# A fused attention and mixing kernel: every engine's order planned by a list scheduler, mixing as filler, long-row loads, V cast on chip

## The chip, the cores and the metric

The kernel runs on one core of a Trainium2 chip. The metric is the device time of one execution in microseconds (us). Beside the timed runs, one execution of each kernel was profiled (span and mean granted clock are on record for every run); its *span* runs from the first to the last instruction and is some 1 to 3 us shorter than the timed runs. Engines: PE does matmuls and transposes, PEld is its weight loading, DVE is the vector engine, ACT the scalar engine, POOL the general engine, SP issues DMA.

## The reference, cut to what matters

Four batches of eight heads, 768 positions, head size 64. Each query sees the three blocks of 64 keys with the best gate score (query times mean key of the block), plus its own block, causally. The attention output goes through a token mixing and a channel mixing.

```python
k_rep = k.reshape(B, H, n_blocks, 64, D).mean(axis=3)
gate_scores = einsum('bhsd,bhnd->bhsn', q, k_rep)            # causal blocks only
mask = top-3 blocks of each query, plus its own block, and causal
attn = softmax(where(mask, q @ k.T / sqrt(D), -1e9)) @ v
x = attn.transpose(0, 2, 1, 3).reshape(B, S, 512)
u = x + (relu(x.T @ w_tok1) @ w_tok2).T                       # token mixing
out = u + relu(u @ w_ch1) @ w_ch2                             # channel mixing
```

In the first tile of 128 queries a query has at most two causal blocks, so top-3 selects all of them: the gates of tile 0 decide nothing.

## The kernel before

Heads are handled in 16 *pairs*, four to a batch. A pair needs: q and k loaded, transposed on PE (fp32) and copied out by ACT; block sums of k and the gate on DVE and PE; the mask, transposed by PE and put beside q; scores, exponential (ACT), multiplication with the diagonal mask (DVE); the product with V ("av") and its normalisation (DVE). When the four pairs of a batch are done, its mixing can run. Each function emits the work of all engines together, and the order of these calls is a fixed interleaving:

```python
preps[0]["trq"](); preps[0]["trk"](); preps[0]["gate"]()
preps[1]["trq"](); preps[0]["mask"](); preps[1]["trk"]()
...
    order = [scores(i, 0, 0)] + stage("gate", i + 1)
    order += [last_av] if last_av else []
    order += [scores(i, 0, 1)] + stage("trq", i + 2) + [scores(i, 0, 2), scores(i, 1, 0)]
    order += stage("mask", i + 1) + [av(i, 0), scores(i, 1, 1)] + stage("trk", i + 2)
    if i + 3 < NP:
        order.append(lambda: load(i + 3))
    order.append(scores(i, 1, 2))
    # the last batch's mixing ("pend") is shared out evenly over the calls of the next four pairs
```

Loads of q and k read one head as rows of 64 fp32 numbers (256 B); V is loaded and converted to fp16 by a DMA that POOL issues:

```python
nc.sync.dma_start(out=t[:, :, 64*g:64*g+64], in_=src[b, h+g].rearrange("(j p) d -> p j d", p=128))
nc.gpsimd.dma_start(out=V16[r][:, g, :, 0:64], in_=v[b, h+g].rearrange("(j p) d -> p j d", p=128))
```

The softmax here doesn't subtract the row's maximum and nothing guards it: scores larger than these inputs give would overflow.

Of the kernel before, what the change touches and what calls it, by code (L numbers as in the profile page):

```python
# [22 lines left out]
WHERE = {kk: (g, off) for g, (_, parts) in enumerate(GROUPS) for kk, off, _ in parts}  # L23


@with_exitstack
def kernel(
# [21 lines left out]
    MASKV = -30000.0  # L49

    sp = ctx.enter_context(tc.tile_pool(name="sb", bufs=1))
    pp = ctx.enter_context(tc.tile_pool(name="ps", bufs=1, space=bass.MemoryType.PSUM))

# [5 lines left out]
    def big(name):  # L59
        return pp.tile([128, 1024], FP, tag="big", bufs=2, name=name)  # L60

    def bank(shape, name, dtype=FP):
        return pp.tile(shape, dtype, tag="bank", bufs=3, name=name)

    pairs = [(b, h) for b in range(B) for h in range(0, H, 2)]
    NP = len(pairs)

    loads = {}

    def load(i):  # L70
        b, h = pairs[i]
        q32 = sp.tile([128, NJ, 128], FP, tag="q32", bufs=3, name=f"q32_{i}")
        k32 = sp.tile([128, NJ, 128], FP, tag="k32", bufs=3, name=f"k32_{i}")
        for t, src in ((q32, q), (k32, k)):
            for g in range(2):
                nc.sync.dma_start(out=t[:, :, 64 * g:64 * g + 64],
                                  in_=src[b, h + g].rearrange("(j p) d -> p j d", p=128))
        r = i % (R + 1)
        for g in range(2):
            nc.gpsimd.dma_start(out=V16[r][:, g, :, 0:64],  # L80
                                in_=v[b, h + g].rearrange("(j p) d -> p j d", p=128))
        loads[i] = (q32, k32)

    R = 3
# [5 lines left out]

    load(0)
    ident32 = const("id32", np.eye(128, dtype=np.float32), FP, nc.scalar)
    for r in range(R):
        nc.vector.memset(ks2[r], 0.0)
        nc.vector.memset(bn16[r], 0.0)
        nc.vector.memset(QA[r][0][64:128, :], 0.0)
        nc.vector.memset(QA[r][1][0:64, :], 0.0)
    for r in range(R + 1):
        nc.vector.memset(V16[r][:, :, :, 64:65], 1.0)
    pidx = np.arange(128)  # L100
    nidx = np.arange(NB)
    jidx = np.arange(NJ)
    mrow = 2 * jidx[None, :, None] + (pidx[:, None, None] >= 64)
    gb1 = (-1.0e6 * np.maximum(0, nidx[None, None, :] - mrow)).astype(np.float32)
    own1 = np.where(nidx[None, None, :] == mrow, 0.0, MASKV).astype(np.float32)
    gbias = const("gbias", np.concatenate([gb1, gb1], axis=2), FP, nc.scalar)
    own = const("own", np.concatenate([own1, own1], axis=2), FP, nc.scalar)
    ident16 = const("id16", np.eye(128, dtype=np.float16), F16, nc.scalar)
    m0_np = (np.arange(128)[None, :] >= np.arange(128)[:, None]).astype(np.float16)
    m0 = const("m0", np.stack([m0_np, m0_np], axis=1), F16, nc.scalar)  # L110
    ind_np = (np.arange(S)[None, :] // 64 == nidx[:, None]).astype(np.float16)
    ind64 = np.zeros((64, S), np.float16)
    ind64[0:NB] = ind_np
    ind_dram = nc.inline_tensor(ind64, name="indc").ap()
    for r in range(R):
        for x in range(2):
            lo = 64 if x == 0 else 0
            nc.sync.dma_start(out=KA[r][x][lo:lo + 64, :], in_=ind_dram)
        if r == 0:
            load(1)  # L120

# [3 lines left out]
    wc2_16 = sp.tile([128, NFC, DM], F16, tag="wc2", name="wc2")  # L125

    def weight_loads():
        w1 = moe_w_tok1.rearrange("(j p) t -> p j t", p=128)
        w2 = moe_w_tok2.rearrange("(g p) s -> p g s", p=128)
        c1 = moe_w_ch1.rearrange("(c p) f -> p c f", p=128)  # L130
        c2 = moe_w_ch2.rearrange("(g p) c -> p g c", p=128)
        th = [lambda: nc.gpsimd.dma_start(out=w1_16, in_=w1), lambda: nc.gpsimd.dma_start(out=w2_16, in_=w2)]
        th += [lambda c=c: nc.gpsimd.dma_start(out=wc1_16[:, c, :], in_=c1[:, c, :]) for c in range(NCC)]
        th += [lambda f=f: nc.gpsimd.dma_start(out=wc2_16[:, f:f + 3, :], in_=c2[:, f:f + 3, :])
               for f in range(0, NFC, 3)]
        return th

    xs = {}

    def prep(i):  # L140
        r = i % R
        st = {}

        def trq():
            q32 = loads[i][0]
            ps = big("tq")
            for j in range(NJ):
                nc.tensor.transpose(out=ps[:, 128 * j:128 * j + 128], in_=q32[:, j, :], identity=ident32)  # L148
            qt = sp.tile([128, S], FP, tag="qt", bufs=2, name=f"qt_{i}")
            nc.scalar.copy(out=qt, in_=ps[:, 0:S])  # L150
            st["qt"] = qt
            nc.gpsimd.tensor_copy(out=QA[r][0][0:64, :], in_=qt[0:64, :])
            nc.gpsimd.tensor_copy(out=QA[r][1][64:128, :], in_=qt[64:128, :])

        def trk():
            k32 = loads[i][1]
            ps = big("tk")
            for j in range(NJ):
                nc.tensor.transpose(out=ps[:, 128 * j:128 * j + 128], in_=k32[:, j, :], identity=ident32)  # L159
            kt = sp.tile([128, S], FP, tag="kt", bufs=2, name=f"kt_{i}")  # L160
            nc.scalar.copy(out=kt, in_=ps[:, 0:S])  # L161
            kst = sp.tile([128, NB], FP, tag="kst", bufs=2, name=f"kst_{i}")
            nc.vector.tensor_reduce(out=kst, in_=kt.rearrange("p (n w) -> p n w", w=64),
                                    axis=AX.X, op=ALU.add)
            nc.vector.tensor_copy(out=ks2[r][64:128, 0:NB], in_=kst[64:128, :])
            nc.vector.tensor_copy(out=ks2[r][0:64, NB:2 * NB], in_=kst[0:64, :])
            nc.gpsimd.tensor_copy(out=KA[r][0][0:64, :], in_=kt[0:64, :])
            nc.gpsimd.tensor_copy(out=KA[r][1][64:128, :], in_=kt[64:128, :])

        def gate():  # L170
            gps = bank([128, NJ, 2 * NB], "gps")
            for j in range(NJ):
                nc.tensor.matmul(out=gps[:, j, :], lhsT=st["qt"][:, 128 * j:128 * j + 128],  # L173
                                 rhs=ks2[r], start=True, stop=True)
            gm = sp.tile([128, NJ, 2 * NB], FP, tag="gm", bufs=2, name=f"gm_{i}")
            m8 = sp.tile([128, NJ, 2, 8], FP, tag="m8", bufs=2, name=f"m8_{i}")
            lt = sp.tile([128, NJ, 2 * NB], FP, tag="lt", bufs=2, name=f"lt_{i}")
            nc.vector.tensor_tensor(out=gm, in0=gps, in1=gbias, op=ALU.add)
            for j in range(NJ):
                for x in range(2):  # L180
                    nc.vector.max(out=m8[:, j, x, :], in_=gm[:, j, NB * x:NB * x + NB])
            nc.vector.tensor_tensor(
                out=lt.rearrange("p j (x n) -> p j x n", n=NB),
                in0=gm.rearrange("p j (x n) -> p j x n", n=NB),
                in1=m8[:, :, :, 2:3].broadcast_to([128, NJ, 2, NB]), op=ALU.is_lt)
            nc.vector.scalar_tensor_tensor(out=lt, in0=lt, scalar=MASKV, in1=own, op0=ALU.mult, op1=ALU.max)
            nc.vector.tensor_copy(out=bn16[r][:, :, :, 0:NB], in_=lt.rearrange("p j (x n) -> p j x n", n=NB))

        def mask():
            bps = bank([128, S], "bps", F16)  # L190
            for j in range(NJ):
                nc.tensor.transpose(out=bps[:, 128 * j:128 * j + 128],  # L192
                                    in_=bn16[r][:, j, :, :].rearrange("p x n -> p (x n)"), identity=ident16)
            nc.vector.tensor_copy(out=QA[r][0][64:64 + NB, :], in_=bps[64:64 + NB, :])  # L194
            nc.vector.tensor_copy(out=QA[r][1][0:NB, :], in_=bps[0:NB, :])

        return dict(trq=trq, trk=trk, gate=gate, mask=mask)

    E = {}

    def scores(i, x, g):
        r = i % R

        def f():
            width, parts = GROUPS[g]
            ps = big("sps")
            for kk, off, nq in parts:
                q0 = 128 * kk
                a = 0
                while a < nq:  # L210
                    n = min(nq - a, 512 - (off + a) % 512)
# [10 lines left out]
        return f  # L222

    def av(i, x):
        b, h = pairs[i]

        def f():
            aps = pp.tile([128, NJ, 65], FP, tag="av", bufs=1, name="aps")
# [93 lines left out]
    pend = []  # L322
# [35 lines left out]
    for _, g in pend:  # L358
        g()
# [30 lines left out]
```

## Time and profile before

| | before |
|---|---|
| time, median | 318.5 us in the first three runs (317.2 to 322.5) |
| span | 316.6 us |
| first scores / first mixing matmul | 28.8 / 81.2 us |
| busy: PE, DVE, ACT, POOL | 280.0, 181.9, 141.4, 86.6 us |

The first lines of the page of the kernel before: the busy time of each engine, then PE, granted clock and DMA in 40 equal slices of the span (tenths; 9 is 90% or more).

```profile
span 316.6 us, 5878 instructions
...
PE 280.0 (88%) x2272; PEld 182.0 (57%) x2272; DVE 181.9 (57%) x624; ACT 141.4 (45%) x185; POOL 86.6 (27%) x110
...
PE   1325888888999999999999999999999999899994
...
PEclk9999598778899999999999999999999999999999
DMA  9999999675444445646324444330000011100022
```

PE is nearly always busy from a quarter of the span on, and mostly idle before. DMA shows the opposite. The table of stretches cuts the execution at the first scores and at the first mixing matmul (columns: stretch, its length, then busy us and instruction count of PE, PEld, DVE, ACT, POOL, then granted PE clock, DMA share, GB/s):

```profile
0.00:28.80 28.80, 9.28 (x43) 7.92 (x44) 8.63 (x37) 3.68 (x4) 13.60 (x22) 1.00 1.20 196
28.80:81.20 52.40, 43.96 (x382) 32.43 (x381) 35.57 (x146) 30.84 (x37) 27.28 (x34) 0.80 1.07 151
81.20:316.60 235.40, 226.75 (x1851) 141.70 (x1848) 137.71 (x442) 106.92 (x145) 45.69 (x56) 1.00 0.29 58
```

In the 28.8 us head PE works 9.3 us. In the attention stretch that follows it is busy 44 of 52.4 us, at a mean clock of 0.80. In the mixing stretch it idles 8.7 of 235 us. The clock of 1.00 listed for the head is doubtful: six fp32 transposes at each of 5.9, 9.9 and 23.4 us took 1.51 to 1.54 us, against 0.85 us at 40.4 us, where 1.00 is listed too. The chain of waits (start, length, what) tells why the head is long and how regular the second stretch is:

```profile
8.39 18.29 DMA k_1_120<-in_k_dram
...
44.45 1.52 PE gps L173 x12
...
55.02 1.52 PE gps L173 x12
...
65.58 1.52 PE gps L173 x12
...
76.12 1.64 PE gps L173 x12
...
81.21 1.29 PE tok_921 L258 x6
```

The chain passes 18.3 us in the load of the second pair's k. PE did pair 1's q transposes (23.4 us) and the first transpose of its k (26.8 us) ahead of pair 0's mask transposes:

```profile
26.81 0.44 PE L159 MATMUL tk<-id_91,k_1_120 128*128 128x128 f32 x1 [1.92 <-DMA k_1_120<-in_k_dram]
27.05 0.84 PE L192 MATMUL bps<-id_113,bn_80 128*128 128x128 f16 x6
```

The calls above have the mask ahead of pair 1's k; why PE took one transpose of it first is not recorded. Behind the head, one gate follows another every 10.6 us, with four pairs to do before mixing can start.

### The profile page before, as it was taken

The page shows a single profiled execution, that of the slowest core. Times are in us where ns is not written, and L with a number is a line of the kernel's source. Part 1 is how long each engine was busy: PE and PEld are TensorE (multiplying, and loading weights), DVE is VectorE, ACT ScalarE, POOL GpSimd, SP SyncE. Part 2 cuts the span into 40 slices and gives each one's busy share as a digit, 9 for nine tenths or more (in the row PEclk, how much of TensorE's full clock was granted, in tenths as well). Part 3 has the DMA queues.
Part 4 walks back from the last instruction along what each step waited for, and adds up shares of the span by engine and source line. Part 5 has one row for each costly group of instructions (what it writes and reads, how often), then busy time and mean ns, then how long its engine had stood idle before and what let it go on. Part 6 is the DMA issues. An engine that isn't in the chain of part 4 may idle for free.

```text
span 316.6 us, 5878 instructions
## 1 busy us (share of the span) xinstructions
PE 280.0 (88%) x2272; PEld 182.0 (57%) x2272; DVE 181.9 (57%) x624; ACT 141.4 (45%) x185; POOL 86.6 (27%) x110
## 2 busy tenths in 40 slices
PE   1325888888999999999999999999999999899994
PEld 1324665667557675656676766566766655456541
DVE  4223478667496666565975657576865644373321
ACT  2104268556465573526556644354666443214200
POOL 7606565444233333333222324140222000000000
PEclk9999598778899999999999999999999999999999
DMA  9999999675444445646324444330000011100022
GB/s 162 213 191 220 195 215 213 100 104 87 65 62 64 62 64 95 131 100 127 52 36 59 70 90 90 81 79 2 0 2 1 2 66 69 65 2 0 0 101 99
DMA packets 83179, 27.23 MB, mean 86 GB/s; under 512 B 76112, under 2 KB 79568, under 8 KB 83152
## 3 DMA queue, kind: packets, MB, share of 16 engines
q1 hardware_dynamic: 54112, 19.47, 26.5%
q0 software_dynamic: 28320, 7.08, 22.6%
q10 hardware_dynamic: 720, 0.31, 0.4%
q8 instruction: 18, 0.29, 0.4%
q14 instruction: 9, 0.07, 0.1%
HBM read 27.64 MB, written 6.29 MB: 107 GB/s over the span
## 4 chain that ended last, share of the span: by engine, by line
PE 76%; DVE 8%; DMA 7%; ACT 5%; issue 1%; ACTq 0%; SPq 0%
PE sps L212 10%; PE gps L173 7%; PE aps L233 6%; DMA k_1_120<-in_k_dram 6%; PE tq L148 3%; PE ups L267 3%; PE tk L159 3%; PE bps L192 2%; DMA id_113<-id16c 2%; DVE u_3626 L269 1%; PE utps L276 1%; PE c_3376 L299 1%; PE c_3925 L299 1%; PE c_3584 L299 1%; PE c_3485 L299 1%
## 5 line engine op out<-in xcount | busy, mean ns | idle before, releaser
L286 PEld LDWEIGHTS <-wc_133 128*128 128x128 f16 x384 | 37.1, 98 | 26.2 <-issue 0.8
L80 POOL DMA_DIRECT2D V_61<-in_v_dram x8 | 6.8, 847 | 23.7 <-PE aps L233 13.2
L212 PE MATMUL sps<-Q_65,K_71 128*128 128x512 f16 (+3 forms) x48 | 11.6, 330 | 0.7 <-ACT e_12_0_2820 L217 0.5
L299 PEld LDWEIGHTS <-h_3_3628 128*128 128x128 f16 x72 | 7.0, 97 | 8.3
L80 POOL DMA_DIRECT2D V_62<-in_v_dram x8 | 6.6, 828 | 18.6 <-PE aps L233 9.2
L80 POOL DMA_DIRECT2D V_64<-in_v_dram x8 | 6.6, 824 | 18.4 <-PE aps L233 11.5
L212 PE MATMUL sps<-Q_66,K_72 128*128 128x512 f16 (+3 forms) x48 | 10.6, 333 | 0.9 <-ACT e_3_1_820 L217 0.5
L299 PEld LDWEIGHTS <-h_2_2826 128*128 128x128 f16 x72 | 6.9, 98 | 7.3
L299 PEld LDWEIGHTS <-h_0_920 128*128 128x128 f16 x72 | 7.0, 98 | 7.2
L299 PEld LDWEIGHTS <-h_1_1873 128*128 128x128 f16 x72 | 7.0, 98 | 7.2
L212 PE MATMUL sps<-Q_68,K_74 128*128 128x512 f16 (+3 forms) x40 | 9.4, 324 | 1.3 <-ACT e_1_1_496 L217 0.5
L80 POOL DMA_DIRECT2D V_63<-in_v_dram x8 | 6.6, 826 | 13.8 <-PE sps L212 7.3
L212 PE MATMUL sps<-Q_69,K_75 128*128 128x512 f16 (+3 forms) x40 | 9.1, 313 | 0.8 <-ACT e_8_0_1867 L217 0.5
L212 PE MATMUL sps<-Q_67,K_73 128*128 128x512 f16 (+3 forms) x40 | 9.4, 322 | 0.5 <-ACT kt_343 L161 0.3
L212 PE MATMUL sps<-Q_70,K_76 128*128 128x512 f16 (+3 forms) x40 | 8.8, 321 | 0.9 <-ACT e_2_1_659 L217 0.5
L194 DVE COPY Q_65<-bps 12x768 f16<-12x768 f16 x6 | 3.3, 555 | 9.5 <-PE bps L192 9.4
L258 PEld LDWEIGHTS <-w_131 128*128 128x128 f16 x48 | 4.6, 98 | 6.1 <-issue 1.0
L212 PEld LDWEIGHTS <-K_72 128*128 128x128 f16 x48 | 4.8, 106 | 4.7 <-issue 2.3
L267 PEld LDWEIGHTS <-w_132 128*128 128x128 f16 x48 | 4.3, 97 | 5.4 <-issue 1.9
L148 PE MATMUL tq<-id_91,q_1_119 128*128 128x128 f32 x6 | 1.5, 425 | 6.2 <-DMA q_1_119<-in_q_dram 6.2
L148 PE MATMUL tq<-id_91,q_0_83 128*128 128x128 f32 x6 | 1.5, 425 | 5.9 <-DMA q_0_83<-in_q_dram 5.9
L212 PEld LDWEIGHTS <-K_71 128*128 128x128 f16 x48 | 4.7, 105 | 3.5 <-issue 1.7
(1023 smaller groups left out, 863.7 us busy)
## 6 DMA issues: line engine op xcount, KB each, us to landing
out_dram<-ob SPq DMA_DIRECT2D x24, 256.0 KB, 2.0
wc_133<-in_moe_w_ch_dram POOLq DMA_DIRECT2D x4, 384.0 KB, 13.6
wc_134<-in_moe_w_ch_dram POOLq DMA_DIRECT2D x4, 384.0 KB, 7.9
V_61<-in_v_dram POOLq DMA_DIRECT2D x8, 96.0 KB, 4.1
V_62<-in_v_dram POOLq DMA_DIRECT2D x8, 96.0 KB, 3.6
V_63<-in_v_dram POOLq DMA_DIRECT2D x8, 96.0 KB, 3.9
V_64<-in_v_dram POOLq DMA_DIRECT2D x8, 96.0 KB, 4.0
q_0_83<-in_q_dram SPq DMA_DIRECT2D x2, 192.0 KB, 3.9
```

The costliest lines, as they stand in the source:

```text
L80: nc.gpsimd.dma_start(out=V16[r][:, g, :, 0:64], in_=v[b, h + g].rearrange("(j p) d -> p j d", p=128))
L148: nc.tensor.transpose(out=ps[:, 128 * j:128 * j + 128], in_=q32[:, j, :], identity=ident32)
L159: nc.tensor.transpose(out=ps[:, 128 * j:128 * j + 128], in_=k32[:, j, :], identity=ident32)
L173: nc.tensor.matmul(out=gps[:, j, :], lhsT=st["qt"][:, 128 * j:128 * j + 128], rhs=ks2[r], start=True, stop=True)
L192: nc.tensor.transpose(out=bps[:, 128 * j:128 * j + 128], in_=bn16[r][:, j, :, :].rearrange("p x n -> p (x n)"), identity=ident16)
L194: nc.vector.tensor_copy(out=QA[r][0][64:64 + NB, :], in_=bps[64:64 + NB, :])
L212: nc.tensor.matmul(out=ps[:, off + a:off + a + n], lhsT=KA[r][x][:, 128 * kk:128 * kk + 128], rhs=QA[r][x][:, q0 + a:q0 + a + n], start=Tr ...
L233: nc.tensor.matmul(out=aps[:, jq, :], lhsT=E[i, x, g][:, o:o + 128], rhs=V16[i % (R + 1)][:, x, kk, :], start=(kk == 0), stop=(kk == jq))
L258: nc.tensor.matmul(out=mp, lhsT=w1_16[:, j, 128 * t:128 * t + 128], rhs=xs[b][:, j, :], start=(j == 0), stop=(j == NJ - 1))
L267: nc.tensor.matmul(out=mp, lhsT=w2_16[:, t, 128 * j:128 * j + 128], rhs=st["h1"][:, t, :], start=(t == 0), stop=(t == 1))
L286: nc.tensor.matmul(out=mp, lhsT=wc1_16[:, cc, 128 * fc:128 * fc + 128], rhs=st["uT"][:, cc, a:e], start=(cc == 0), stop=(cc == NCC - 1))
L299: nc.tensor.matmul(out=mp, lhsT=st["h2"][:, fc, 128 * j:128 * j + 128], rhs=wc2_16[:, fc, :], start=(fc == 0), stop=(fc == NFC - 1))
```

## The change

Its intent is to keep PE busy everywhere. All work is described as operations with an engine, a duration, dependencies, buffers and a priority; a list scheduler plans the order of every engine before anything is emitted. Attention has priority, mixing (priority 1000 and up) fills PE whenever attention isn't ready. Beside this:

- q and k of the first four pairs are loaded in long rows (six consecutive positions, 1536 B) and reordered on chip by DVE (k) and POOL (q);
- V is loaded as fp32 by SP and converted to fp16 by a POOL copy;
- gates, top-3 and mask of tile 0 are dropped;
- block sums are put in place by a reduction rather than by a copy; the indicator rows (constant rows beside k, 1 where a position belongs to a block, against which the mask beside q is multiplied) shrink from 64 to 12; the rings (sets of buffers used in turn) of Q and K have four places, not three; 14 scratch matmuls warm PE at the start.

```diff
+AHEAD = 2.5
+R = 4
+LONG = 4
+def plan(ops, rings, near=60.0):            # list scheduler, cut
+            t0 = min(t for t, _ in lst)
+            pick = min((x for x in lst if x[0] <= t0 + near), key=lambda x: (x[1].prio, x[0]))
...
+                if i < LONG:
+                    eng.dma_start(out=t[:, g, :, :], in_=src[b, h + g].rearrange("(p j) d -> p j d", j=NJ))
...
-        nc.gpsimd.dma_start(out=V16[r][:, g, :, 0:64], in_=v[b, h + g].rearrange("(j p) d -> p j d", p=128))
+                nc.sync.dma_start(out=t[:, g, :, :], in_=v[b, h + g].rearrange("(j p) d -> p j d", p=128))
+            nc.gpsimd.tensor_copy(out=V16[i % (R + 1)][:, :, :, 0:D], in_=T["v32", i])
...
-            for j in range(NJ):
-                nc.tensor.matmul(out=gps[:, j, :], lhsT=st["qt"][:, 128 * j:128 * j + 128],
+            for j in range(GJ):                                   # GJ = NJ - 1
+                nc.tensor.matmul(out=g[:, j, :], lhsT=T["qt", i][:, 128 * j + 128:128 * j + 256],
...
+        base = 10.0 * i                       # priorities of attention
+        fill = 1000.0 * (b + 1)               # priorities of mixing
+    order, span = plan(ops, RINGS)
+        for o in order:
+            o.fn()
```

## The prediction

> **What bounds the kernel now.** The page has PE busy 280.0 of 316.6 us; the table of stretches puts most idle time early: PE is busy 10.4 of the first 30 us and 0.88 of 40-84 us, at a granted clock of 0.61 to 1.00. From 100 to 260 us it is over 92% busy. (a) Head: the first scores start at 28.8 us. The chain of waits runs 18.3 us through the load of pair 1's k, because PE's fixed order puts pair 0's mask transposes (inputs ready at 19.5) behind that pair. DMA moves some 200 GB/s for 55 us; 76112 of 83179 packets are under 512 B. The Trainium skill ("DMA: Bandwidth & Descriptors", Specifications) asks for 512 B for line rate. (b) Attention without filler: gates come every 10.6 us (44.5 to 76.1 in the chain) though a pair has about 6.5 us of PE and 8.4 of DVE work. The first mixing matmul is at 81.2 us. (c) 235 us of mixing at 65.4 us a batch against 63.6 of summed matmuls, and 4 for the last output.
>
> **Costs of the change** (durations from timeline and groups). PE: mixing 37.6 us a batch, attention 6.5 us a pair; without tile 0's gates and mask 6.2: 250 us for 254. DVE: 7.2 us a pair for 8.4 (kcopy 0.85 to 0.35, five tiles of six, no separate cast), plus a reorder of 0.4 to 0.8 in four pairs. POOL loses 32 V issues of 0.83 us and gains 16 casts of about 0.8: neutral. DMA: q and k of four pairs go from 12288 packets of 256 B to 2048 of 1536 B; V moves from the software queue (51 ns a packet in the first 60 us) to the hardware queue (24 ns).
>
> **Head.** Memsets come first (DVE until about 7.5 us at 0.38 each), so transposes start near 8.5, not 5.9. But pair 0 then waits for nobody: first scores at about 17 us.
> **Attention without filler.** The new PE order again puts all four pairs before the first mixing matmul. From 17 us until then DVE has about 38 us of work (five preparations of 4.0, four pairs of 3.4, reorders, gaps), ACT 28, PE 28: DVE bounds it, first mixing matmul at about 57 us instead of 81.
> **Rest.** 218 of PE's 250 us remain, plus 6-8 of small stalls, plus 4 at the end: span 285-287. The order ends with about 100 us of mixing alone, so attention ends near 180; until then DVE is about 90% busy, and the plan assumes faster DVE operations than the trace shows (output add 0.60 against 0.70), so PE may stall.
>
> Runs lie 2 us above the span: **287 us, range 278 to 298**; faster by over 2% 0.96, within 2% 0.03, slower 0.01. Of 31 us, 24 come before the first mixing matmul, 4 from dropped PE work.
>
> **Right if**: first scores at 15-19 us; first mixing matmul at 52-61, DVE over 85% busy before it and PE clock still dipping (the Trainium skill, "TensorE: Matmul & The Clock Gate", Part 1: a PE found idle gets half clock; the trace agrees); from there to the end 226-234 us; PE busy 265-270.
> **Wrong if**: DMA delivers pairs 4-6 too late for the fixed order; indicator loads, which wait for POOL's memsets, hold pair 1's loads beyond 14 us; POOL casts slow DVE's copies; or a saturated DVE makes PE wait more than 8 us after 57.

## The result, and the profile after

The changed kernel took 287.59 us (median of 4 runs, 287.12 to 290.34) against 319.7 us for the kernel before in the same rounds. The ratio is 0.9009, 95% interval 0.8937 to 0.908. Ratios here are the mean time of one kernel's fast runs over that of the other's of the same rounds, so not quite the ratio of the medians quoted. The same lines of the page of the changed kernel:

```profile
span 286.2 us, 5839 instructions
...
PE 267.7 (94%) x2238; PEld 171.2 (60%) x2238; DVE 177.2 (62%) x586; ACT 143.6 (50%) x185; POOL 83.0 (29%) x106
...
PE   7488877899999999999999999999999999999994
...
PEclk9867999999999999999999999999999999999999
DMA  4799999999940896891111000001110003100032
```

and the same three stretches, cut at its own first scores (18.3 us) and first mixing matmul (58.9 us):

```profile
0.00:18.30 18.30, 11.87 (x54) 7.17 (x55) 11.07 (x43) 4.31 (x4) 13.74 (x21) 0.85 0.75 208
18.30:58.90 40.60, 33.67 (x366) 25.11 (x367) 33.58 (x134) 31.94 (x36) 28.02 (x36) 0.94 1.13 213
58.90:286.20 227.30, 222.14 (x1820) 138.91 (x1818) 132.58 (x411) 107.36 (x146) 41.22 (x50) 1.00 0.32 77
```

Of the 30.4 us between the spans, 10.5 come from the head (28.8 to 18.3), 11.8 from the attention stretch (52.4 to 40.6) and 8.1 from the mixing stretch (235.4 to 227.3). In the last, PE has 4.6 us less to do (226.75 to 222.14) and idles 3.5 us less (8.65 to 5.16). What is left there is mostly the 4 us after PE's end.

The timeline of the new head, some lines of PE and DVE and one of POOL (start, length, engine, line, operation; in brackets the idle time before it and what ended it), shows what bounds it now:

```profile
7.59 0.87 PE L270 MATMUL tk<-id,k 128*128 128x128 f32 x6 [0.86 <-DVE k L245]
...
10.80 1.28 PE L316 MATMUL gps<-ks,qt 128*128 128x24 f32 x10 [1.65 <-ACT qt L282]
...
13.53 0.58 DVE L245 COPY k<-kl 128x768 f32<-128x768 f32 x1 [2.88 <-DMA kl<-in_k_dram]
...
14.04 0.27 DVE L324 TENSOR_TENSOR gm<-gps,gbias 128x120 f32<-128x120 f32 x1
...
14.26 1.51 PE L270 MATMUL tk<-id,k 128*128 128x128 f32 x6 [2.19 <-DVE k L245]
...
14.97 0.82 POOL L245 COPY q<-ql 128x768 f32<-128x768 f32 x1 [1.26 <-DMA ql<-in_q_dram]
...
16.30 0.71 PE L359 MATMUL bps<-id,bn 128*128 128x128 f16 x5 [0.53 <-DVE bn L348]
...
18.26 1.01 PE L380 MATMUL sps<-Q,K 128*128 128x512 f16 x3
```

Pair 0's gates run at 10.8 us and end at 12.1. The wait is on DVE: its planned order has the reorder of pair 1's k ahead of the next step of pair 0's gates (`gm`). DVE idles 2.88 us until that k lands at 13.5, and only then runs `gm`, at 14.0. PE transposes pair 1's k at 14.3; the mask and the first scores of pair 0 follow. So pair 0 still waits for pair 1, by some 2 us; before, its mask was ready at 19.5 us and transposed at 27.1. The six transposes at 14.26 took 1.51 us, those at 7.59 0.87: PE's clock had halved, which the experiments return to.

### The profile page after: what moved, and what is told of

It reads as the page before. It is cut to its first block, busy times and chain, and to the rows that moved or that the text cites. A ratio compares the mean times of both kernels' runs of the same rounds, so it can differ in the third digit from the quotient of the medians.

```text
span 286.2 us, 5839 instructions
## 1 busy us (share of the span) xinstructions
PE 267.7 (94%) x2238; PEld 171.2 (60%) x2238; DVE 177.2 (62%) x586; ACT 143.6 (50%) x185; POOL 83.0 (29%) x106
## 4 chain that ended last, share of the span: by engine, by line
PE 79%; DVE 8%; DMA 3%; ACT 3%; POOL 2%; issue 2%; SPq 1%; ACTq 0%; POOLq 0%
PE c L508 22%; PE c L487 21%; PE sps L380 10%; PE aps L409 6%; PE gps L316 5%; PE tok L440 4%; PE tq L270 3%; PE ups L452 3%; DMA ql<-in_q_dram 3%; PE tk L270 3%; DVE e L398 2%; PE bps L359 2%; ACT e L391 1%; PE utps L468 1%; DVE m L333 1%
## 5 line engine op out<-in xcount | busy, mean ns | idle before, releaser
L391 ACT ACTIVATE e<-sps 128x1024 f16<-128x1024 f32 (+1 forms) x96 | 84.6, 918 | 24.9 <-PE sps L380 23.6
L487 PE MATMUL c<-uT,wc 128*128 128x256 f16 (+1 forms) x384 | 66.2, 326 | 0.1
L508 PE MATMUL c<-wc,h 128*128 128x512 f16 x288 | 64.6, 379 | 0.0
L380 PE MATMUL sps<-Q,K 128*128 128x512 f16 (+3 forms) x256 | 49.0, 309 | 3.5 <-ACT e L391 1.4
L497 ACT ACTIVATE h<-c 128x512 f16<-128x512 f32 x48 | 28.7, 598 | 46.9 <-PE c L487 46.3
L487 PEld LDWEIGHTS <-wc 128*128 128x128 f16 x384 | 37.1, 98 | 23.7 <-issue 0.5
L508 PEld LDWEIGHTS <-h 128*128 128x128 f16 x288 | 27.5, 98 | 31.7
L290 POOL CAST K<-kt 64x768 f16<-64x768 f32 x32 | 26.8, 836 | 61.1 <-ACT kt L280 58.1
L398 DVE TENSOR_TENSOR e<-e,m 128x256 f16<-128x256 f16 x96 | 32.6, 351 | 8.8 <-ACT e L391 8.1
L409 PE MATMUL aps<-V,e 128*128 128x65 f16 x672 | 27.5, 194 | 1.0 <-DVE e L398 0.9
L316 PEld LDWEIGHTS gps<-ks,qt 128*128 128x128 f32 x160 | 19.5, 192 | 5.3 <-ACT qt L282 3.0
L428 DVE TENSOR_TENSOR x<-aps,rc 128x384 f16<-128x384 f32 x32 | 17.7, 555 | 0.9
L367 DVE COPY Q<-bps 12x640 f16<-12x640 f16 x32 | 15.5, 484 | 2.7 <-PE bps L359 2.1
```

The costliest lines, as they stand in the source:

```text
L290: nc.gpsimd.tensor_copy(out=dst[i % R][x][lo:lo + 64, :], in_=T[name, i][lo:lo + 64, :])
L316: nc.tensor.matmul(out=g[:, j, :], lhsT=T["qt", i][:, 128 * j + 128:128 * j + 256], rhs=ks2[i % R], start=True, stop=True)
L380: nc.tensor.matmul(out=p[:, off + a:off + a + n], lhsT=KA[i % R][x][:, 128 * kk:128 * kk + 128], rhs=QA[i % R][x][:, q0 + a:q0 + a + n], s ...
L391: nc.scalar.activation(out=e[:, 0:width], in_=T["sps", i, x, g][:, 0:width], func=AF.Exp, scale=scale)
L398: nc.vector.tensor_tensor(out=d, in0=d, in1=m0, op=ALU.mult)
L409: nc.tensor.matmul(out=p[:, jq, :], lhsT=T["e", i, x, g][:, o:o + 128], rhs=V16[i % (R + 1)][:, x, kk, :], start=(kk == 0), stop=(kk == jq))
```

## The experiments

Each kernel below is the changed kernel with one edit, correct in its results, timed in three rounds (the last one in five) against the kernel before. "First mixing" is the start of the first token-mixing matmul in the profile.

| run | ratio to before | span | first scores | first mixing | stretch behind it |
|---|---|---|---|---|---|
| the changed kernel | 0.9009 | 286.2 | 18.3 | 58.9 | 227.3 |
| oldorder | 1.1039 | 348.0 | 20.7 | 85.0 | 263.0 |
| oldorder2 | 1.0918 | 347.5 | 20.5 | 86.8 | 260.7 |
| long0 | 0.9139 | 291.4 | 17.8 | 59.5 | 231.9 |
| gate0 | 0.9297 | 295.9 | 18.2 | 64.6 | 231.3 |
| vdma | 0.9424 | 298.5 | 24.2 | 78.3 | 220.2 |
| dve_plus | 0.9123 | 288.1 | 18.3 | 60.8 | 227.3 |
| act_plus | 0.9103 | 288.2 | 18.3 | 60.9 | 227.3 |
| pool_plus | 0.9106 | 288.2 | 18.4 | 60.9 | 227.3 |
| pe_plus | 0.9113 | 289.2 | 19.1 | 61.9 | 227.3 |
| keepwarm | 0.9064 | 286.6 | 19.3 | 59.3 | 227.3 |
| head | 0.9081 | 287.6 | 17.7 | 60.3 | 227.3 |
| head2 | 0.8998 | 283.2 | 15.5 | 55.8 | 227.4 |

### The order alone: oldorder and oldorder2

The scheduler was replaced by the call order of the kernel before, everything else kept:

```diff
-    order, span = plan(ops, RINGS)
+    order = []          # filled pair by pair: scores, gates, av, scores, trq, ... as in the kernel before
+    loads(0); loads(1); tr(0, "q32"); tr(0, "k32"); gates(0); tr(1, "q32"); masks(0); tr(1, "k32"); loads(2)
+    for i in range(NP):
+        put(("v", i))   # V's cast; in oldorder2: put(("v", i + 2)), two pairs ahead
```

> The changed kernel with all its parts, but every engine's order taken from the static interleaving of the kernel before instead of from the list scheduler. Theory A (the order makes the gain: it lets DVE set the pace of the attention phase and fills PE later): gates come about 10.5 us apart again until the first mixing matmul, which moves from 59 to 70-76 us; time 298-306 us. Theory B (the new parts make it: long rows, V cast, fewer gates, warm PE, smaller constants): first mixing matmul within 3 us of 59, time 286-292 us. Theory C (DMA limits the first 60 us): little change too, 286-292 us.

Measured: 351.48 us, 10% slower than the kernel before. The new V cast has no place in the old order, and mine was a bad one: the waits of SP's queue showed 113 us for V buffers that POOL had not freed, with q's loads behind them. So the second try:

> The order of the kernel before once more, but with V's cast placed two pairs ahead: in the first try V's loads sat on the SP queue waiting 113 us in sum for a V buffer, and q's loads waited behind them, so it did not measure the order. If the order itself carries the gain: no waits of SP's queue for V casts, first mixing matmul at 68-80 us, mixing stretch as in the kernel before (about 235 us), time 302-318 us. If the parts carry it: 286-295 us.

Measured: 348.65 us. The waits for V buffers fell from 113 to 18 us and the time hardly moved; both expectations missed. The chain of waits of oldorder2 now passes through POOL's queue instead:

```profile
24.61 3.04 DMA v<-in_v_dram
28.54 0.84 POOL q L245
29.42 1.56 PE tq L270 x6
...
46.39 8.50 DMA v<-in_v_dram
```

POOL stands in order on a V cast whose data is still coming (3.0 and 8.5 us); behind it stand the reorder of q and the casts, and behind those PE, whose granted clock was 0.50 on average from 20 to 40 us. What follows: with these new parts the old order, as these two tries fill it, is no smaller gain but a loss of 29 us, so the parts alone don't bring the gain. What doesn't follow is how much the order is worth by itself: both tries contain a cast that the old order had no place for, and the kernel before with a scheduler alone was not built.

### Long rows: long0

```diff
-LONG = 4
+LONG = 0
```

> The changed kernel with q and k of every pair loaded in 256 B rows again (LONG = 0), no reorders; the order is planned anew. Theory A: pair 0's and pair 1's data land later, first scores 3 to 6 us later than 18.3, but four reorders of 0.6 us leave DVE; first mixing matmul at 60-64 us, time 289-293 us. Theory C (DMA limits the attention phase; its busy share is over 1.0 from 10 to 80 us): 10240 more packets at 24 ns over 16 engines are 15 us of DMA, first mixing matmul at 68 us or later, time 296 us or more.

Measured: 291.87 us (289.26 to 293.21), ratio 0.9139, span 5.2 us longer. The median is what theory A said, the way there is not: first scores came 0.5 us *earlier* (no reorder between pair 0's load and its transpose), and the loss sits behind the first mixing matmul. The new plan had done less by then (393 matmuls against 419), PE then had 225.4 us of work instead of 222.1 and idled 6.6 us instead of 5.2. DMA was late about as rarely as in the changed kernel: PE waited 3.7 us for pair 1's k and POOL 1.2 us for V, where DVE and POOL of the changed kernel waited 2.9, 1.3 and 0.5 us. How much long rows and the plan that comes of them are worth is not clear of noise. The medians are 4.3 us apart, but the intervals of the ratios overlap (0.9048 to 0.9229 against 0.8937 to 0.908), and the profiled run was long0's slowest, at a mean clock of 0.968. At a mean clock of 0.982 long0 has spans of 287.5 and 288.4 us, the changed kernel 286.2. The first scores are not where they help, and rows and plan were not separated.

### Gates of tile 0: gate0

```diff
-    GJ = NJ - 1
+    GJ = NJ             # and the slices of gate, mask and put start at tile 0 again; same planned order
```

(The warming tile was halved in width, with twice the matmuls, to make room in memory.)

> The changed kernel with gates, top-3 and mask of tile 0 put back, same order. Theory A: PE gains 0.25 us a pair, of which about 11 pairs lie in the stretch where PE is never idle: time up by 2.5 to 4 us, to 290-292; first mixing matmul up to 1.5 us later. If PE were not the bound after 59 us: below 1 us.

Measured: 296.97 us (294.72 to 297.7), span 9.7 us longer, of which 4.0 lie behind the first mixing matmul and 5.7 before it. Of the 4.0, 3.6 us are PE work (225.70 against 222.14 us) of the ten pairs whose gates lie there, so 0.36 us a pair and not 0.25. The 5.7 had not been expected. The stretches from 12 to 20 and 20 to 28 us of this kernel and of the changed one (columns as above; the third from the right is the granted clock):

```profile
12.00:20.00 8.00, 5.09 (x25) 3.49 (x24) 5.33 (x22) 2.69 (x3) 5.11 (x7) 0.58 1.11 304
20.00:28.00 8.00, 7.09 (x35) 6.00 (x35) 4.94 (x20) 3.86 (x5) 4.86 (x6) 0.57 1.20 224
```

```profile
12.00:20.00 8.00, 4.63 (x22) 3.10 (x21) 5.56 (x20) 2.46 (x3) 5.00 (x7) 0.57 1.10 295
20.00:28.00 8.00, 6.79 (x48) 5.51 (x49) 6.45 (x22) 5.53 (x6) 6.95 (x8) 0.79 1.20 218
```

With tile 0 in, PE stays at about half clock for all of 20 to 28 us and is busy 7.1 of 8 us while it does fewer matmuls (35 against 48). That this is the cause of the 5.7 us is not shown, and the other runs speak against the clock as the whole cause: gate0's fastest run had a mean granted clock of 0.988 and a span of 293.0 us, the two runs of the changed kernel at 0.988 had 285.2 and 285.3. So 7.7 of the 9.7 us remain at an equal mean clock, 3.7 more than the 4.0 behind the first mixing matmul. DVE has 2.0 us more work in the attention stretch of gate0 (35.6 against 33.6 us); what the rest is stays open.

### V through POOL's converting DMA: vdma

```diff
-                nc.sync.dma_start(out=t[:, g, :, :], in_=v[b, h + g]...)      # and the cast on POOL
+                nc.gpsimd.dma_start(out=V16[i % (R + 1)][:, g, :, 0:D], in_=v[b, h + g]...)
```

> The changed kernel with V loaded by POOL's converting DMA again and no cast on POOL; planned anew. Theory A: neutral for time, 286-290 us, first mixing matmul at 57-61. Theory C: V's packets take 51 ns instead of 24 ns, 10 pairs of 1536 packets over 16 engines are some 20 us more DMA in the first 60 us: first mixing matmul at 64 us or later, time 293 us or more.

Measured: 300.78 us (299.29 to 301.7), span 12.3 us longer. Theory A's "neutral" is wrong. POOL's timeline at the head of vdma:

```profile
7.25 6.70 POOL L253 DMA_DIRECT2D V<-in_v_dram  x8 [0.26 <-DVE V L690]
13.99 0.82 POOL L245 COPY q<-ql 128x768 f32<-128x768 f32 x1
```

Eight V issues of 0.84 us each stand before the reorder of pair 0's q, so first scores start at 24.2 us, 5.9 us later. The Trainium skill ("TensorE: Matmul & The Clock Gate", the table at the top) says that POOL's queue is strict first in, first out; this trace agrees: the reorder runs the moment the eighth issue is done. The plan put them there because nothing in its model holds an issue back. Theory C came nearer to the size, but the waits don't bear out its reason: in the first 90 us no engine but DVE (1.3 us, once) is seen waiting for a DMA, although DMA's share is above 1. The rest of the delay (first mixing 19.4 us later, while 105 more matmuls are done before it and the stretch behind is 7.1 us shorter) was not taken apart: the plan differs.

### Which engine bounds the attention stretch: four kernels with extra work

Each adds 24 pieces of about 0.3 us (36 matmuls for PE) to one engine before the first mixing matmul, on no data path, in the same planned order (in pool_plus five of the 24 come before the first scores):

```diff
 # dve_plus, behind each diagonal multiply        # act_plus, behind each exponential
+    if i < 4: nc.vector.memset(warm, 0.0)         +    if i < 4: nc.scalar.copy(out=warm[:, 0:312], in_=warm[:, 0:312])
 # pool_plus, behind each q or k cast             # pe_plus, ahead of each group of scores
+    if i < 6: nc.gpsimd.memset(warm[:, 0:320], 0) +    the first 512-column score matmul 1 or 2 times more
```

> The changed kernel, same order, with 24 scratch memsets of about 0.28 us on DVE, one after each diagonal multiply of pairs 0 to 3: about 7.5 us more DVE work before the first mixing matmul, on no data path. Theory A (DVE bounds the attention phase): first mixing matmul 5 to 8 us later (64-67 us), time 292-296 us. Theory D (no engine bounds it, the chain of waits between engines does, with all of them about 80% busy): about a third, 1 to 4 us.

> The same with 24 scratch copies of about 0.33 us on ACT, one after each exponential of pairs 0 to 3 (about 7.9 us). Theory A: ACT has slack (79% busy), first mixing matmul 0 to 2 us later. Theory D: 2 to 5 us, as much as for DVE.

> The same with 24 scratch memsets of about 0.32 us on POOL, one after each q or k cast of pairs 0 to 5 (about 7.7 us). Theory A: POOL is 69% busy, first mixing matmul 0 to 1.5 us later. Theory D: 1 to 3 us.

> The same with 36 score matmuls of 512 columns repeated in pairs 0 to 3 (36 x 0.216 = 7.8 us of PE). Theory A: PE is 83% busy at a clock that is not always full, first mixing matmul 0 to 3 us later. Theory D: 2 to 5 us. Should all four of these kernels move it by less than 2 us, DMA bounds the phase (theory C).

Measured: 290.9, 289.93, 290.21 and 290.56 us. The attention stretch of the four, in this order, from each one's first scores (in pe_plus from 18.3 us, where the first added matmul starts, 0.8 us ahead of the scores) to its first mixing matmul (columns: stretch, length, busy us of PE, PEld, DVE, ACT, POOL, clock, DMA share, GB/s):

```profile
18.30:60.80 42.50, 33.65 (x366) 25.31 (x367) 38.92 (x158) 31.45 (x36) 28.25 (x36) 0.96 1.12 204
```

```profile
18.30:60.90 42.60, 34.18 (x367) 25.35 (x368) 33.57 (x134) 38.87 (x60) 28.11 (x36) 0.95 1.09 210
```

```profile
18.40:60.90 42.50, 34.96 (x368) 26.66 (x368) 33.22 (x134) 32.15 (x36) 35.02 (x55) 0.91 1.08 207
```

```profile
18.30:61.90 43.60, 39.22 (x402) 27.54 (x403) 35.26 (x134) 32.41 (x36) 27.75 (x36) 0.99 1.13 212
```

Against 40.6 us in the changed kernel (DVE 33.6, ACT 31.9, POOL 28.0, PE 33.7 us busy), DVE's busy time rose by 5.3 us and the stretch by 1.9; ACT 6.9 and 2.0; POOL 7.0 and 1.9; PE 5.5 and 3.0. Three of them passed on about a third of what was added and PE about half, whatever their busy share (69% to 83%). The stretch behind is 227.3 us in all four. In timed runs the means lie 2.1 to 2.8 us above that of the changed kernel; only dve_plus's interval (from 0.909) is clear of the changed kernel's (to 0.908), the others' begin at 0.907. The differences between the four are within the noise of single profiles, and their clocks differ (0.91 to 0.99 against 0.94; pe_plus, at 0.99, did its other work faster, so more than 5.5 us was added). So no single engine bounds the attention stretch. That fits theory D, a chain that passes from engine to engine in a fixed order. Theory A's claim for DVE falls: 5 to 8 us were expected. Theory C's own mark, all four below 2 us, is missed only by PE's 3.0, the other three moved the first mixing matmul by 1.9 to 2.0. What speaks against it is the list of waits: between 18.3 and 58.9 us no engine of the changed kernel is seen waiting for a DMA.

### PE's clock and the head: keepwarm, head, head2

```diff
 # keepwarm
+            if o is O["gate", 0]:      # 11 scratch matmuls of 512 columns into a spare bank
 # head: pair 1's loads ahead of the indicator loads of ring places 1 to 3; memsets of places 2 and 3 later
+            if o is O["k32", 0]: clear_dve(2)
+            if o is O["kcopy", 0]: clear_dve(3)
+            if o is O["cast", "kt", 0, 1]: clear_pool(2)
+            if o is O["cast", "qt", 0, 1]: clear_pool(3); indicators(1); indicators(2); indicators(3)
 # head2: as head, but the memsets of K go to ACT before its first copy, and 7 + 4 + 4 scratch matmuls
 #        stand behind pair 0's q transposes, pair 0's gates and pair 1's k transposes
```

> The changed kernel, same order, with 11 scratch matmuls of 512 columns put behind the gates of pair 0, where PE is idle from 12.1 to 14.3 us waiting for pair 1's k. Theory E (that idle gap halves PE's clock from 12 to 20 us and again to 27 us, and work at half clock lengthens the chain of pair 0 and 1): granted clock 1.0 from 12 to 20 us, first scores at 17.3-18, first mixing matmul 2 to 4 us earlier, time 284-286 us. Theory F (the clock does not matter, the chain is made of DVE, ACT and POOL times and of the late load): no change within 1 us.

> The changed kernel, planned order unchanged, but pair 1's loads come ahead of the indicator loads of ring places 1 to 3 on the SP queue, and the memsets of ring places 2 and 3 come after the first reorder and later. Theory: pair 1's k lands near 10 us instead of 13.5, the first reorder starts near 5 instead of 6.9, PE has no gap at 12-14 us: first scores at 14-16 us instead of 18.3, first mixing matmul 2.5 to 4.5 us earlier, the stretch behind it unchanged at 227 us, time 283-285 us. If the attention phase has a floor of its own (DMA delivering pairs 4 to 6, theory C): first mixing matmul less than 1 us earlier although the scores start earlier.

Measured: keepwarm 289.39 us (287.42 to 291.54), head 289.44 (289.28 to 291.2): neither differs from the changed kernel beyond noise, and both missed what they were built for. In keepwarm the clock fell all the same, and earlier, so that it tests neither theory E nor F:

```profile
10.00:11.00 1.00, 0.21 (x2) 0.22 (x3) 0.60 (x3) 0.72 (x1) 0.94 (x2) 1.00 1.22 265
11.00:12.00 1.00, 1.00 (x9) 1.00 (x9) 0.00 (x0) 0.00 (x0) 0.90 (x3) 0.78 0.89 270
12.00:13.00 1.00, 1.00 (x4) 0.51 (x5) 0.00 (x0) 0.00 (x0) 0.94 (x2) 0.50 0.96 297
```

It halved between 11 and 12 us, before the gap that the scratch matmuls were to fill, although PE's longest idle time until then was 1.65 us. The scratch matmuls then ran at half clock and pushed pair 1's k to 16.0 us and first scores to 19.3. Still, first mixing came at 59.3: the start moved by 1 us, its end by 0.4.

In head, pair 1's k was ready earlier (transposed at 11.9 instead of 14.3 us), but the memsets that I had put between POOL's casts and V's cast made q's reorder the next thing that PE waited for (1.9 us). First scores came only 0.5 us earlier, and the clock stood at half until 26 us:

```profile
12.00:20.00 8.00, 4.34 (x22) 2.91 (x22) 4.61 (x18) 2.82 (x3) 7.37 (x10) 0.53 0.79 222
20.00:28.00 8.00, 6.92 (x36) 5.70 (x36) 5.42 (x21) 4.22 (x5) 5.24 (x7) 0.62 1.23 234
```

The last kernel mends both:

> The mended head: as head, but the memsets of ring places 2 and 3 for K go to ACT, idle from 3.4 to 7.2 us, instead of between POOL's casts, where they and V's cast made pair 1's q reorder late (PE waited 1.9 us for it); and 15 scratch matmuls in three places keep PE from standing idle between 7.9 and 13.8 us, where head fell to half clock from 12.8 to 26 us. Planned order unchanged. Expected if the start of pair 0 and PE's clock set the attention phase together: granted clock 1.0 until at least 16 us, first scores at 15-16.5 us, first mixing matmul at 55.5-57.5, stretch behind it 227.3, time 284.5-286.5 us (1% below the changed kernel). Expected if the phase is a chain that the earlier start does not shorten: first scores earlier but first mixing matmul at 58-60 us, time 287-289.5.

Measured: 286.17 us (284.92 to 288.25, 6 runs), ratio 0.8998 (0.8946 to 0.9051). The same two stretches:

```profile
12.00:20.00 8.00, 6.10 (x46) 4.40 (x47) 6.86 (x35) 4.39 (x5) 7.08 (x9) 1.00 0.82 234
20.00:28.00 8.00, 6.56 (x84) 5.26 (x83) 7.85 (x28) 6.22 (x8) 7.61 (x11) 1.00 1.15 213
```

In this profile the clock stays at 1.00, first scores come at 15.5 us and first mixing at 55.8, so the earlier start is carried to the end: the span is 283.2 us, 3.0 below the changed kernel. The attention stretch takes 40.3 us at full clock, against 40.6 at a mean of 0.94. That does not show that a faster PE gains little, because data came late in the middle of head2's stretch. POOL stood 7.5 us for V, and the chain of waits passes 9.3 us through the load of a later pair's k:

```profile
33.98 9.28 DMA k<-in_k_dram
...
40.65 0.90 POOL L260 CAST V<-v 128x768 f16<-128x768 f32 x1 [7.48 <-DMA v<-in_v_dram]
```

The first of these lines is from the chain of waits, the second from POOL's timeline. What this cost was not taken apart (PE itself had only just become free when that k landed).

What the clock is worth can be estimated from the repeats of one and the same kernel. The changed kernel's spans were 285.2 and 285.3 us at a mean granted clock of 0.988, 286.2 at 0.982 and 288.6 at 0.970; keepwarm's went from 285.6 at 0.994 to 289.0 at 0.976. A line through the runs of the changed kernel and its twelve variants, with a level for each, gives an estimate of 1.8 us of span for 0.01 of mean clock. As 0.01 of 286 us is 2.9 us of PE time, some 0.6 us of span is lost for each us that PE loses. This is a correlation between runs, not an experiment. But head2's gain goes with the clock: its two runs at 0.980 and 0.981 had spans of 286.4 us, no better than the changed kernel at 0.982.

In timed runs head2 is the fastest kernel by median, but its interval overlaps that of the changed kernel, so that it beats it is not shown by time.

## Why the prediction was right or wrong

The total was right: 287 us predicted, 287.59 measured, in part by luck, as the third step shows. The steps:

- **Bounds before, head.** Right: first scores at 18.3 us, "15-19" predicted. But "pair 0 then waits for nobody" is wrong. It waits about 2 us for pair 1's k; the load stands behind the indicator loads and those behind POOL's memsets, as one of the "wrong if" points had feared; it landed at 13.5 us, within the 14 allowed.
- **First mixing matmul at about 57 us**: 58.9, within "52-61".
- **"DVE bounds it"**: this step failed. DVE was busy 83% there, not over 85%, and 5.3 us more DVE work cost 1.9 us, where a stretch bound by DVE would have grown by 5.3. The 38 us of work in the prediction were 33.6 of work and 7.0 of idle time. That 40 us were predicted from 17 to 57 us, and 40.6 measured, is luck: the overestimate of DVE's work came close to the waits that had been left out.
- **PE clock still dipping**: right, 0.94 on average and 0.57 from 12 to 20 us. But PE's idle time alone, which the prediction names, does not explain such dips: in the kernel before, PE was busy 7.0 of the 8 us from 38 to 46 us, and then the clock fell to 0.66 (46 to 48 us) and 0.50 (48 to 50 us).
- **Mixing stretch 226-234 us**: 227.3. **PE busy 265-270**: 267.7. Dropped work of 4 us: PE's busy time in that stretch fell by 4.6.
- **DVE 90% busy until attention ends, PE might stall**: the first part is wrong (93.9 of 119.6 us from 59.0 to 178.6 us, 79%), so nothing came of the second: PE was busy 119.1 of those 119.6 us. Attention ended at 178.6, "near 180".
- **V's move "neutral"**: mis-sized. Undone, it costs 12.3 us of span, first of all because POOL issues V's loads one after another ahead of pair 0's q.
- **Dropped gates worth 4 us**: mis-sized. Undone, they cost 9.7 us of span: 4.0 behind the first mixing matmul, where ten of the 16 pairs' gates lie, and 5.7 before it.
- **24 of 31 us before the first mixing matmul**: 22.3 of 30.4.

The parts can't be added up: the span differences on undoing gates (9.7), V cast (12.3), long rows (5.2) or the order (61) sum to far more than 30 us. That each part was fitted to the plan of the others is a likely reason, not one that a run shows. What exactly makes the old order so slow with the new parts stays open.

## What to carry to other kernels

When extra work on any of four engines lengthens a stretch, but on each by only a third to a half of what was added, no single engine bounds it, and a busy share of 83% does not make one the bound: taking load off it may give no larger share back (no run here tried that). In the one profile where the chain started 2.8 us earlier and PE's clock stayed full (head2), 3.1 us reached the end of the stretch; but the same kernel at a lower clock was no faster than the kernel it was made from. So look at the clock of each run before explaining a difference of one or two per cent. A scheduler's order and the parts it orders belong together; a new operation put into a fixed in-order queue at a guess can cost more than all that it saves. And what a planner's model does not hold back (here V's loads on POOL, free to issue from the start) it can put at a bad place: in vdma ahead of pair 0's q.

## What the Trainium skill lacked or had wrong

- "TensorE: Matmul & The Clock Gate", "Why this matters for your kernels": it advises no PE idle gaps over about 3 us. That is not enough: in keepwarm the clock halved between 11 and 12 us after no gap longer than 1.65 us. In the 4 us before, PE had run only transposes and gate matmuls of 24 columns; Part 4 of the page says that transposes don't count as busy in the same way, which would fit. With scratch matmuls that left no gap over 0.42 us between 6.4 and 15.5 us it stayed at 1.00 in head2's profile.
- "DMA: Bandwidth & Descriptors", Specifications: 512 B or more for line rate, but the page gives no rate measured on trn2 for loads in shorter rows. From 13.5 to 24 us long0, with 256 B rows for q, k and V (9132 of 9133 packets under 512 B), moved 219 GB/s; the changed kernel, with rows of 1536 B for a part of them (5629 of 6709 under 512 B), 290 GB/s.
- Same page, "Anatomy of one DMA — SWDGE (gpsimd) path": it calls the generation of descriptors small and says that many can be emitted before the cost shows. On POOL each V issue of 768 rows took 0.84 us, eight took 6.7 us, and POOL's own copies stood behind them (vdma).
